# Token-list writes without order among themselves, and the early index reads moved ahead of the last batch's writes

## Chip, core and metric

The kernel runs on one core of a Trainium2 chip. The metric is the device time of one execution in microseconds (us); three runs of the kernel before are known, and their median is compared with the median of the changed kernel. The engines are named as in the profile: PE (matmul), PEld (its weight load), DVE (VectorE), ACT (ScalarE), POOL (GpSimd), SP (SyncE, which here only issues transfers). SPq and POOLq are the sequencers of SP and POOL.

## What is computed

Attention in two steps, a dense layer, and a mixture of eight experts of which every token takes one:

```python
p_packed = sm_attn(p, k, v)                    # 8 batches, 8 heads, 576 tokens, head_dim 64
x = sm_attn(q, p_packed, p_packed)             # -> x of shape (4608, 512)
h = x @ w_in ; x = (h - tanh(h)) @ w_out       # w_in 512x2048, w_out 2048x512
logits = x @ w_gate                            # 8 experts
e_idx = argmax(logits, axis=1)
for e in range(8):
    mask = e_idx == e
    ye = relu(x[mask] @ w1[e]) @ w2[e]         # w1 512x1024, w2 1024x512
    out[mask] = gate_w[mask, None] * eom[mask, e, None] * ye
```

## The kernel before

A first part packs keys and values. Then 16 half batches of 288 tokens (`halves`) go through attention and the dense layer, one after the other on PE: `up` (first matrix), `up_b`, `down` (second matrix), 16 steps `f` each. What belongs beside this is put into a table by `at(i, f, function)`: it is emitted in the program behind step `f` of half batch `i`, and every engine works its share strictly in that order. So (15, 4) is behind step 4 of the last half batch, and calls with the same place keep the order in which they were entered.

While half batch `i` is on PE, the half batch before it is routed: `logits` to `rank` find each token's expert and its rank there; `place` (15 of 16 at step 5; the last one after the loop) computes where each token stands in its expert's list and writes the token numbers to `tab`, a table in DRAM with 4608 places for each expert. It does so with three indirect transfers from POOL (L610), 96 numbers of four bytes each, after DVE has made the addresses `ix` (L608). One step later `gate_b` scales the rows and sends them from `x2s` to `x2d` in DRAM by four transfers from SP (L634).

When the last half batch is under way, the expert with most tokens so far is known (`favour`), and its weights are fetched (`early_fetch`, `early_split`). Its first three tiles of 128 tokens are the early tiles 0, 1, 2. `gather` brings a tile in: SP loads the tile's offset (L783), then reads 128 token numbers from `tab` into `ixt` (L785); POOL gathers the 128 rows from `x2d` into `xg` (L788), for which there are two buffers. `early_gather` for tiles 0 and 1 stands at (15, 8), and for tile 2 at (15, 14) behind `x_up` of tile 0, in which PE transposes `xg` (L815). The reads take only lists that `place` had filled up to the half batch before.

After the loop, PE works the early tiles (`mm1`, `h_up`, `mm2`) while the last half batch is routed and placed. `listing` then makes the offsets `of_i` (L920) of all other tiles ("m" 0, 1, ...) on DVE; `gather` of tile m0 follows, and `x_up` of m0 stands in PE's order behind `mm2` of tile 1. A tile's result is copied to `y` (L865, one buffer) and written out by an indirect transfer from POOL (L867). Every tile up to the end is worked in this order; the weights of an expert that changes are fetched by `refetch` and split by `resplit`, both under a condition.

Of the kernel before, what the change touches and what calls it, by code (L numbers as in the profile page):

```python
# [8 lines left out]
F32 = mybir.dt.float32  # L9
# [3 lines left out]
U32 = mybir.dt.uint32  # L13
# [6 lines left out]
NB, NH, S, D = 8, 8, 576, 64  # L20
# [3 lines left out]
NT = NB * S  # L24
# [5 lines left out]
EARLY = 3  # L30
# [14 lines left out]
def attention_moe_kernel(ctx: ExitStack, tc: tile.TileContext, q, k, v, p, w_in, w_out, w_gate, w_og, w1, w2, out):  # L45
    nc = tc.nc
    vec, act, pool, pe, sp = nc.vector, nc.scalar, nc.gpsimd, nc.tensor, nc.sync
# [3 lines left out]
    tab = dram.tile([TROWS, 1], I32, name="tab")  # L51
# [3 lines left out]
    def open_pool(name, bufs=1, side="left", space=None):  # L55
        kw = {"space": space} if space is not None else {"side": side}
        kw["reuse_waits"] = "tile"
        pl = tc.alloc_tile_pool(name=name, bufs=bufs, **kw)
        pools.append(pl)
        return pl  # L60
# [6 lines left out]
    const = open_pool("const")  # L67
# [2 lines left out]
    base_e = const.tile([1, NE], F32, name="base_e")  # L70
    iota_e = const.tile([1, NE], F32, name="iota_e")
    quad = const.tile([128, 1], F32, name="quad")

    ef = open_pool("ef")
    w_in_sb = ef.tile([128, 4, DFF], F32, name="w_in_sb")
# [8 lines left out]
    tok = cab.tile([96, 2 * NB, 3], I32, name="tok")  # L84
# [228 lines left out]
    with ExitStack() as pa:  # L313
# [107 lines left out]
        for a in range(4):  # L421
            r = slice(32 * a, 32 * a + 32)
# [53 lines left out]
    with ExitStack() as pb:  # L476
# [117 lines left out]
        def place(b, hf):  # L594
            n = HB * NE
            pr_, oh = tmp["pr"], tmp["oh"]
            vec.tensor_copy(seg[:, :, 1:], pr_[:, n:2 * n].rearrange("p (t e) -> p e t", e=NE))
            so = tmp['rt'].tile([128, NE, HB + 1], F32, name="so")
            vec.tensor_tensor_scan(so.rearrange("p e t -> p (e t)"), smask.rearrange("p e t -> p (e t)"), seg.rearrange("p e t -> p (e t)"), 0.0, ALU.mult, ALU.add)
            pos = tmp['rt'].tile([128, HB, NE], F32, name="pos")  # L600
            vec.tensor_tensor(pos, pr_[:, :n].rearrange("p (t e) -> p t e", e=NE), so[:, :, 0:HB].rearrange("p e t -> p t e"), op=ALU.add)
            vec.tensor_copy(seg[:, :, 0:1], so[:, :, HB:HB + 1])
            vec.tensor_tensor(pos, pos, oh, op=ALU.mult)
            ps = tmp['rt'].tile([128, HB], F32, name="ps")
            vec.tensor_reduce(ps, pos, axis=AX.X, op=ALU.add)
            ix = tmp['rt'].tile([96, 3], I32, name="ix")
            for r in range(3):
                vec.tensor_copy(ix[32 * r:32 * r + 32], ps[32 * r:32 * r + 32, 3 * r:3 * r + 3])  # L608
            for j in range(3):
                pool.indirect_dma_start(tab, bass.IndirectOffsetOnAxis(ap=ix[:, j:j + 1].bitcast(U32), axis=0), tok[:, 2 * b + hf, j:j + 1], None)  # L610

        def gate(b, hf):
            oh, ex, lg = tmp["oh"], tmp["lex"], tmp["lg"]
# [26 lines left out]
        def at(i, f, fn, *a):  # L640
            i, f = divmod(NF * i + f, NF)
            todo.setdefault((i, f), []).append((fn, a))
# [11 lines left out]
        for i, (b, hf) in enumerate(halves):  # L654
            n = b + 1
            if i:
                p_ = halves[i - 1]
                at(i, 0, logits)
                at(i, 1, logits_b)
                at(i, 2, choose_a)  # L660
                at(i, 3, choose_b)
                at(i, 4, rank)
                at(i, 5, place, *p_)
                at(i, 5, gate, *p_)
                at(i, 6, gate_b, *p_)
# [37 lines left out]
        st = {}  # L703
# [75 lines left out]

        plain = {0, 1, 2, ("m", 0), ("m", 1)} | {("m", n) for n in range(NMAIN + 2, NSTEP)}  # L780

        def gather(key, off, rows=NT + 1):
            r = sp.value_load(off, min_val=0, max_val=TROWS - 128)  # L783
            ix = const.tile([128, 1], I32, name="ixt", bufs=6)
            sp.dma_start(ix, tab[bass.ds(r, 128)].rearrange("(j g) o -> g j o", g=4))  # L785
            xg = st["cg"].tile([128, 4, 128], F32, name="xg", bufs=2)
            if key in plain:
                pool.indirect_dma_start(xg.rearrange("p c n -> p (c n)"), None, x2d[:rows], bass.IndirectOffsetOnAxis(ap=ix.bitcast(U32), axis=0))  # L788
            else:
                iq = const.tile([128, 4], I32, name="iq", bufs=3)  # L790
                sp.dma_start(iq, tab[bass.ds(r, 128)].rearrange("(j g) o -> j (g o)", g=4).unsqueeze(0).broadcast_to([4, 32, 4]))
                pool.tensor_scalar(iq, iq, 4.0, quad, op0=ALU.mult, op1=ALU.add)
                src = x2d[:rows].rearrange("n (q c) -> (n q) c", q=4)
                for g in range(4):
                    pool.indirect_dma_start(xg[:, g], None, src, bass.IndirectOffsetOnAxis(ap=iq[:, g:g + 1].bitcast(U32), axis=0))  # L795
            st["g", key] = xg, ix

        def early_gather(n):
            gather(n, st["eo"][:, n:n + 1], NT - S)

        def open_gather():
            close(rt)
# [177 lines left out]
        for n, f in enumerate((13, 15, 17, 19, 20, 23, 26, 28)):  # L980
            if n < 2:
                at(14, 10, early_fetch, n)
            at(14, f, early_split, n)
            if n + 2 < 8:
                at(14, f, early_fetch, n + 2)
        at(15, 7, open_gather)
        at(15, 8, early_gather, 0)
        at(15, 8, early_gather, 1)
# [82 lines left out]
        for n in range(NMAIN):  # L1071
            s = n % 2
            key = "m", n
# [20 lines left out]
        for n in range(NMAIN, NSTEP):  # L1094
            key = "m", n
# [48 lines left out]
```

## Time and profile before

| | |
|---|---|
| median of 3 runs | 1365.23 us (1360.34 to 1365.89) |
| profiled execution: its time / its span | 1369.21 us / 1367.3 us |
| mean granted clock of TensorE in it | 0.963 of full speed |
| PE busy | 1265.3 us, 93% of the span |
| PEld busy | 1082.4 us, 79% |
| DVE busy | 816.1 us, 60% |
| ACT busy | 530.1 us, 39% |
| POOL busy | 327.9 us, 24%, 363 instructions |

PE is the busiest engine, and in the page's forty slices it is busy for nine tenths or more from the seventh to the thirty-ninth, with one gap: two slices of 8 and 6 tenths, somewhat behind the middle of the span. That gap is where the half batches end and the early tiles begin. Busy time is an average over stages; the rows further down show what PE waits for in that gap.

### The profile page before, as it was taken

How to read it: one execution, taken by the hardware profiler on the slowest of the kernel's cores; microseconds unless marked ns; L12 is line 12 of the kernel's file. 1: busy time of each engine (PE TensorE's matmuls, PEld its weight loads, DVE VectorE, ACT ScalarE, POOL GpSimd, SP SyncE). 2: the span in 40 equal slices, each digit the busy share in tenths (PEclk: the TensorE clock that was granted, in tenths of full speed). 3: DMA queues.
4: the chain of work that ended last, by engine and by line, in shares of the span. 5: the costliest groups of instructions: out<-in, count | busy, mean ns of one | idle time of the engine just before them, and what ended most of it. 6: DMA issues, size and time to landing. Idle time of an engine off the chain costs nothing. (4 is left out here: it accounts for less than half of the span.)

```text
span 1367.3 us, 25742 instructions
## 1 busy us (share of the span) xinstructions
PE 1265.3 (93%) x9024; PEld 1082.4 (79%) x9024; DVE 816.1 (60%) x1811; ACT 530.1 (39%) x1141; POOL 327.9 (24%) x363
## 2 busy tenths in 40 slices
PE   6575879999999999999999999869999999999997
PEld 5354668998989989889899899757888778788775
DVE  3755996777776777768677777363233533443551
ACT  4555434443434344343434435332222422332431
POOL 3313760000000000000000000115444444454431
PEclk7878889999999999999999999989999999999999
DMA  8999421122111221122103023331113311332441
GB/s 227 242 246 207 138 64 22 15 36 36 27 19 27 36 30 24 19 36 36 26 11 53 19 47 112 117 80 39 44 47 101 105 46 45 113 100 73 131 154 41
DMA packets 140354, 102.24 MB, mean 75 GB/s; under 512 B 97296, under 2 KB 121876, under 8 KB 139572
## 3 DMA queue, kind: packets, MB, share of 16 engines
q1 hardware_dynamic: 130516, 80.33, 25.5%
q0 software_dynamic: 9696, 20.14, 4.8%
q8 instruction: 74, 1.21, 0.4%
q14 instruction: 68, 0.56, 0.2%
HBM read 215.60 MB, written 19.57 MB: 172 GB/s over the span
## 5 line engine op out<-in xcount | busy, mean ns | idle before, releaser
L610 POOL DMA_INDIRECT tab<-tok,ix x48 | 45.3, 943 | 641.5 <-DVE ix L608 460.7
L517 ACT ACTIVATE gh<-gg 128x288 fp32r<-128x288 f32 x256 | 112.6, 440 | 153.2 <-PE acc L532 68.0
L518 DVE TENSOR_TENSOR gl<-gg,gh 128x288 fp32r<-128x288 f32 x244 | 109.9, 450 | 96.9 <-ACT gh L517 90.6
L531 PE MATMUL acc<-gl,wo_bt 128*128 128x288 f32 x512 | 154.9, 303 | 11.5 <-DVE gl L518 7.0
L851 DVE TENSOR_TENSOR hl<-pt,hh 128x512 fp32r<-128x512 f32 x76 | 52.3, 690 | 185.4 <-ACT hh L850 174.2
L504 PE MATMUL ph<-a_hi,wf_hi 128*128 128x288 f32 x512 | 160.5, 314 | 0.9 <-DVE gg L510 0.5
L506 PE MATMUL ph<-a_hi,wf_lo 128*128 128x288 f32 x512 | 152.7, 298 | 3.9 <-DVE wf_lo L228 3.9
L531 PE MATMUL acc<-gl,wo_a 128*128 128x288 f32 x512 | 152.8, 298 | 3.7 <-POOL gl L518 3.7
L795 POOL DMA_INDIRECT xg<-x2d,iq x132 | 138.4, 1049 | 64.5 <-issue 57.0
L530 PE MATMUL acc<-gh,wo_a 128*128 128x288 f32 x512 | 152.1, 297 | 1.8 <-ACT pp L298 1.8
L532 PE MATMUL acc<-gh,wo_bt 128*128 128x288 f32 x512 | 152.8, 298 | 0.0
L530 PE MATMUL acc<-gh,wo_bt 128*128 128x288 f32 x512 | 152.7, 298 | 0.0
L505 PE MATMUL ph<-a_lo,wf_hi 128*128 128x288 f32 x512 | 152.3, 297 | 0.0
L532 PE MATMUL acc<-gh,wo_a 128*128 128x288 f32 x512 | 152.3, 297 | 0.0
L510 DVE TENSOR_TENSOR gg<-ph,th 128x288 f32<-128x288 f32 x256 | 115.9, 453 | 55.6 <-ACT th L508 54.3
L839 ACT ACTIVATE h<-ph 128x512 f32<-128x512 f32 x76 | 45.3, 598 | 241.1 <-PE ph L838 205.3
L508 ACT ACTIVATE th<-ph 128x288 f32<-128x288 f32 x256 | 104.1, 406 | 78.8 <-PE ph L506 77.7
L504 PEld LDWEIGHTS ph<-a_hi,wf_hi 128*128 128x128 f32 x512 | 97.3, 190 | 43.4 <-issue 38.6
L860 PE MATMUL py<-w2h,hh 128*128 128x512 f32 x304 | 127.0, 418 | 0.2
L861 PE MATMUL py<-w2l,hh 128*128 128x512 f32 x304 | 121.1, 398 | 1.7 <-DVE w2l L765 1.7
L837 PE MATMUL ph<-w1l,xh 128*128 128x512 f32 x304 | 121.2, 399 | 1.4 <-DVE w1l L765 1.0
L862 PE MATMUL py<-w2h,hl 128*128 128x512 f32 x304 | 120.8, 397 | 0.0
(223 smaller groups left out, 2756.8 us busy)
## 6 DMA issues: line engine op xcount, KB each, us to landing
raw<-in_moe_w_dram SPq DMA_DIRECT2D x37, 2048.0 KB
sraw<-in_moe_w_dram SPq DMA_DIRECT2D x37, 1024.0 KB
x2s<-in_moe_w_dram SPq DMA_DIRECT2D x37, 1024.0 KB
kt<-in_k_dram SPq DMA_DIRECT2D x16, 576.0 KB
vt<-in_v_dram SPq DMA_DIRECT2D x48, 192.0 KB
x2d<-x2s SPq DMA_DIRECT2D x64, 144.0 KB
qt<-in_q_dram SPq DMA_DIRECT2D x240, 36.0 KB
st<-in_moe_w_in_dram SPq DMA_DIRECT2D x16, 512.0 KB
```

The lines of the kernel that those rows point to most:

```text
L504: pe.matmul(ph, lhsT=wf_hi[n][:, g, c], rhs=ah[:, g], start=g == 0, stop=False)
L505: pe.matmul(ph, lhsT=wf_hi[n][:, g, c], rhs=al[:, g], start=False, stop=False)
L506: pe.matmul(ph, lhsT=wf_lo[n][:, g, c], rhs=ah[:, g], start=False, stop=g == 1)
L510: vec.tensor_tensor(gg, ph, th, op=ALU.subtract)
L530: pe.matmul(acc[j], lhsT=hi[:, j], rhs=gh, start=f == 0, stop=False)
L531: pe.matmul(acc[j], lhsT=hi[:, j], rhs=gl, start=False, stop=False)
L532: pe.matmul(acc[j], lhsT=lo[:, j], rhs=gh, start=False, stop=f == NF - 1)
L795: pool.indirect_dma_start(xg[:, g], None, src, bass.IndirectOffsetOnAxis(ap=iq[:, g:g + 1].bitcast(U32), axis=0))
L837: pe.matmul(ph, lhsT=xh[:, c], rhs=w1l[:, c, r], start=False, stop=False)
L860: pe.matmul(py, lhsT=hh[:, c], rhs=w2h[:, c], start=c == 0, stop=False)
L861: pe.matmul(py, lhsT=hh[:, c], rhs=w2l[:, c], start=False, stop=False)
L862: pe.matmul(py, lhsT=hl[:, c], rhs=w2h[:, c], start=False, stop=c == 7)
```

## The change

Two things are changed. The 48 transfers that write `tab` are declared free of order among themselves, each with a one-element `memset` of a scratch tile ahead of it on POOL; a read of `tab` is made to wait for all writes that came before it in the program. And the offsets and token numbers of the three early tiles are read by `early_index` at (15, 4), ahead of the `place` at (15, 5), and no longer inside `early_gather`, which only gathers now.

```diff
+    gap = const.tile([1, 1], F32, name="gap")
...
             for j in range(3):
-                pool.indirect_dma_start(tab, bass.IndirectOffsetOnAxis(ap=ix[:, j:j + 1].bitcast(U32), axis=0), tok[:, 2 * b + hf, j:j + 1], None)
+                pool.memset(gap, 0.0)
+                apart(pool.indirect_dma_start(tab, bass.IndirectOffsetOnAxis(ap=ix[:, j:j + 1].bitcast(U32), axis=0), tok[:, 2 * b + hf, j:j + 1], None))
+
+        listed = []
+
+        def apart(ins):
+            ins = ins.ins
+            if listed:
+                tc.declare_no_dep(ins, group="tab", reason="places of their own")
+            tc.add_to_no_dep_group("tab", ins)
+            listed.append(ins)
+
+        def read_list(ins):
+            for m in listed:
+                tc.add_manual_dep(ins.ins, m.name, mybir.DependencyInfo(mybir.DependencyClass.Sync, mybir.DependencyReason.DATA), reason="all places are written")
+            listed[:] = []
...
-        def gather(key, off, rows=NT + 1):
+        def early_index(n):
+            st["r", n] = read_index(st["eo"][:, n:n + 1])
+
+        def read_index(off):
             r = sp.value_load(off, min_val=0, max_val=TROWS - 128)
             ix = const.tile([128, 1], I32, name="ixt", bufs=6)
-            sp.dma_start(ix, tab[bass.ds(r, 128)].rearrange("(j g) o -> g j o", g=4))
+            got = sp.dma_start(ix, tab[bass.ds(r, 128)].rearrange("(j g) o -> g j o", g=4))
+            if listed:
+                read_list(got)
+            return r, ix
+
+        def gather(key, off, rows=NT + 1):
+            r, ix = read_index(off) if off is not None else st["r", key]
...
         def early_gather(n):
-            gather(n, st["eo"][:, n:n + 1], NT - S)
+            gather(n, None, NT - S)
...
+        for n in range(EARLY):
+            at(15, 4, early_index, n)
         at(15, 7, open_gather)
         at(15, 8, early_gather, 0)
```

How the instructions stand on the two engines that issue these transfers follows, in the program's order. A wait on DMASW or DMAHW is one for a transfer from POOL or from SP, on one of eight counters that are used in turn; DVE, PE and Pool are waits for those engines.

On POOL, before, around the `place` of the last half batch but one (the first three lines), the early gathers, and the last `place`:

```order
L610 DMA tab<-tok,ix 36992x1 [waits DMASW3_49,DVE_49]
L610 DMA tab<-tok,ix 36992x1 [waits DMASW4_49]
L610 DMA tab<-tok,ix 36992x1 [waits DMASW5_49]
L788 DMA xg<-x2d,ixt 128x512 [waits DMAHW4_49,DMAHW3_49,DMAHW5_49,DMAHW2_49,DMAHW6_49,DMAHW1_49,DMAHW7_49,DMAHW0_49,Activation_49]
...
L788 DMA xg<-x2d,ixt 128x512 [waits DMAHW2_49,DMASW7_49,PE_49]
...
L610 DMA tab<-tok,ix 36992x1 [waits DMASW6_49,DVE_49]
L610 DMA tab<-tok,ix 36992x1 [waits DMASW2_49]
L610 DMA tab<-tok,ix 36992x1 [waits DMASW3_49]
L788 DMA xg<-x2d,ixt 128x512 [waits DMAHW5_49,DMAHW1_49,DMAHW6_49,DMAHW0_49,DMAHW7_49,DMASW0_49,PE_49]
L867 DMA out_dram<-y,ixt 4608x512 [waits DVE_49]
```

The same place on POOL in the changed kernel:

```order
L612 DMA tab<-tok,ix 36992x1 [waits DMAHW3_49,DMAHW4_49,DMASW4_49,DMAHW5_49,DMASW3_49,DVE_49]
L611 MEMSET gap 1x1 [waits Pool_49]
L612 DMA tab<-tok,ix 36992x1 [waits DMASW5_49]
L611 MEMSET gap 1x1 [waits Pool_49]
L612 DMA tab<-tok,ix 36992x1 [waits DMASW6_49]
L814 DMA xg<-x2d,ixt 128x512 [waits DMAHW2_49,DMAHW1_49,DMAHW6_49,DMAHW0_49,DMAHW7_49,DMASW7_49,Activation_49]
...
L612 DMA tab<-tok,ix 36992x1 [waits DMASW2_49,DVE_49]
L611 MEMSET gap 1x1 [waits Pool_49]
L612 DMA tab<-tok,ix 36992x1
L611 MEMSET gap 1x1 [waits Pool_49]
L612 DMA tab<-tok,ix 36992x1 [waits DMASW4_49]
L814 DMA xg<-x2d,ixt 128x512 [waits DMAHW1_49,DMAHW5_49,DMAHW0_49,DMAHW6_49,DMASW5_49,DMAHW7_49,DMASW0_49,PE_49]
```

Before, the second and third write each wait for the counter of the write just ahead of them. Afterwards a write that names a DMASW counter names that of a transfer of an earlier half batch or tile, since the counters go round; the first write of the last half batch but one now also waits for the three index reads (DMAHW3 to 5).

On SP, before, from the second last weight fetch of the early tiles to the first index read:

```order
L760 DMA sraw<-in_moe_w_dram 128x2x512 [waits DMAHW2_49,DMAHW0_49,DVE_49]
L634 DMA x2d<-x2s 32x9x128 [waits DMAHW3_49,DVE_49]
L634 DMA x2d<-x2s 32x9x128 x3
L760 ISA
L760 DMA sraw<-in_moe_w_dram 128x2x512 [waits DMAHW1_49,DVE_49]
L783 TENSOR_LOAD eo [waits DVE_49]
L783 ISA x2
L785 REGISTER_ALU
L785 DMA ixt<-tab 128x1x1 [waits DMASW6_49,DMASW0_49]
```

And in the changed kernel:

```order
L777 DMA sraw<-in_moe_w_dram 128x2x512 [waits DMAHW2_49,DMAHW0_49,DVE_49]
L803 TENSOR_LOAD eo [waits DVE_49]
L803 ISA x2
L805 REGISTER_ALU
L805 DMA ixt<-tab 128x1x1 [waits DMASW5_49,DMASW4_49,DMASW6_49,DMASW3_49,DMASW7_49,DMASW2_49,DMAHW3_49,DMASW1_49,DMASW0_49]
...
L651 DMA x2d<-x2s 32x9x128 [waits DVE_49]
L651 DMA x2d<-x2s 32x9x128 x2
L651 DMA x2d<-x2s 32x9x128 [waits DMAHW1_49]
L777 ISA
L777 DMA sraw<-in_moe_w_dram 128x2x512 [waits DMAHW2_49,DVE_49]
```

The three loads and index reads (the other two read the same but for their waits and are left out) now stand ahead of the row transfers of the last half batch but one, and the first of them waits for all writes of the list up to the half batch before that.

## Rows read from the trace of the kernel before

**Rows 1.** Timeline of PE: start, length in us, instruction; in brackets idle before, and releaser.

```profile
868.88 1.10 PE L815 MATMUL px<-ident,xg 128*128 128x128 f32 x4 [4.75 <-DMA xg<-x2d,ixt]
...
916.90 1.13 PE L815 MATMUL px<-ident,xg 128*128 128x128 f32 x4 [10.32 <-DMA xg<-x2d,ixt]
...
934.22 0.39 PE L838 MATMUL ph<-w1h,xl 128*128 128x512 f32 x1
```

**Rows 2.** Stretches: length, busy PE, PEld, DVE, ACT, POOL, granted clock, DMA share, GB/s.

```profile
868.00:874.60 6.60, 5.72 (x21) 5.36 (x22) 2.53 (x5) 2.25 (x5) 1.76 (x5) 0.50 0.50 122
...
908.90:922.30 13.40, 5.40 (x15) 4.20 (x16) 2.43 (x3) 4.11 (x5) 4.00 (x4) 0.50 0.44 157
966.00:978.00 12.00, 12.00 (x58) 9.86 (x57) 3.90 (x6) 2.92 (x5) 4.95 (x6) 1.00 0.16 45
```

**Rows 3.** Waits of SP's queue, 835 to 862 and then 895 to 912: total, times, longest.

```profile
SPq L785 <- DMA tab<-tok,ix: 9.6, 1, 9.6
...
SPq L634 <- DVE gl L518: 6.8, 1, 6.8
...
SPq L785 <- DMA tab<-tok,ix: 5.8, 1, 5.8
```

**Rows 4.** Timeline of SP: transfers as issued.

```profile
848.48 2.02 SPq L634 DMA_DIRECT2D x2d<-x2s  x4
...
862.01 4.59 SPq L785 DMA_DIRECT2D ixt<-tab  x3
...
905.75 0.64 SPq L785 DMA_DIRECT2D ixt<-tab  x1
```

**Rows 5.** Instructions of L785 on SP, 895 to 912: ns min/median/max, first and last start.

```profile
L785 SPq MOVE ixt<-tab x2: 29/34/38, 899.9 to 909.7; - x2
```

**Rows 6.** Timeline of POOL: its transfers.

```profile
639.53 0.91 POOL L610 DMA_INDIRECT tab<-tok,ix  x1 [8.96 <-DMA tab<-tok,ix]
...
844.70 0.92 POOL L610 DMA_INDIRECT tab<-tok,ix  x1 [25.14 <-DVE ix L608]
849.33 1.77 POOL L610 DMA_INDIRECT tab<-tok,ix  x1 [3.72 <-DMA tab<-tok,ix]
857.62 0.92 POOL L610 DMA_INDIRECT tab<-tok,ix  x1 [6.51 <-DMA tab<-tok,ix]
865.31 0.99 POOL L788 DMA_INDIRECT xg<-x2d,ixt  x1 [6.78 <-DMA ixt<-tab]
...
889.76 0.93 POOL L610 DMA_INDIRECT tab<-tok,ix  x1 [18.18 <-DVE ix L608]
894.19 0.93 POOL L610 DMA_INDIRECT tab<-tok,ix  x1 [3.50 <-DMA tab<-tok,ix]
900.99 0.91 POOL L610 DMA_INDIRECT tab<-tok,ix  x1 [5.87 <-DMA tab<-tok,ix]
910.49 0.99 POOL L788 DMA_INDIRECT xg<-x2d,ixt  x1 [8.60 <-issue]
911.79 1.01 POOL L867 DMA_INDIRECT out_dram<-y,ixt  x1 [0.31 <-issue]
913.11 0.98 POOL L788 DMA_INDIRECT xg<-x2d,ixt  x1 [0.30 <-issue]
```

**Rows 7.** Groups of POOL by line: busy us, mean ns, idle before.

```profile
L395 POOL MEMSET quad<- 32x1 f32 x4 | 0.4, 92 | 0.1
```

**Rows 8.** Timeline of DVE.

```profile
904.79 2.34 DVE L765 TENSOR_TENSOR w1l<-raw,w1h 128x1024 fp32r<-128x1024 f32 x2
...
918.43 0.69 DVE L865 COPY y<-py 128x512 f32<-128x512 f32 x1 [10.11 <-DMA out_dram<-y,ixt]
...
925.88 0.69 DVE L865 COPY y<-py 128x512 f32<-128x512 f32 x1 [5.01 <-PE py L862]
...
927.62 2.36 DVE L765 TENSOR_TENSOR w2l<-x2s,w2h 128x1024 fp32r<-128x1024 f32 x2
...
933.08 0.68 DVE L823 TENSOR_TENSOR xl<-px,xh 128x512 fp32r<-128x512 f32 x1
```

## The prediction

> **What bounds the kernel now.** I read the timeline of PE first, because PE is the busiest engine. In the second half it waits long at two places only, both the transpose that opens a tile: 4.75 us before early tile 0, and 10.32 us before tile m0, each released by the gather of `xg` [rows 1]. [...] The two waits therefore cost about 4.75 + 2.86 = 7.6 us and 10.32 + 2.70 = 13.0 us. Further on PE has no room: in the row from 966 to 978 it is busy for all 12.00 us at clock 1.00 [rows 2], and the order of the work there does not depend on the list's writes. I take it that what PE gains at the two places reaches the end.
>
> Then the chain behind each wait. POOL's timeline shows the three writes of a half batch in a row, each behind the landing of the one before: 844.70, 849.33, 857.62, and 889.76, 894.19, 900.99 [rows 6]. SP's own waits show who stands behind them: the index read of early tile 0 waited 9.6 us for the writes, that of m0 5.8 us [rows 3]. The reads went out at 862.01 and 905.75 [rows 4], the gathers at 865.31 and 910.49 [rows 6], and PE went on at 868.88 and 916.90.
>
> **The first wait.** The three early reads no longer stand behind the writes of the last half batch but one. They go into SP's queue after a weight fetch, ahead of the row transfers of 848.48. There SP waited 6.8 us for DVE before those transfers [rows 3], that is from about 841.7. Three reads with the two loads between them took 4.59 us, 0.64 of it the last read [rows 4]; so read and load take (4.59 - 0.64) / 2 = 1.98 us, a load alone 1.3, and the three with the first load 5.9 us, inside the 6.8. If that cover were gone, the row transfers would go out late by the excess.
>
> The reads push the first write on POOL, which now waits for them. The third read goes out at about 847; from a read's issue to the gather that uses it took 3.30 us in one case and 4.74 in the other [rows 4, 6], so the writes start at 850 to 852 and not at 844.70, and the third is issued by 855. Nothing reads the list between there and the last half batch. The gather of tile 0 stands next on POOL. Its buffer lies where the routing scratch was, so it still waits for the row transfers of 848.48 to land. That landing has no row; the list write of 849.33, which ran beside them, landed at 857.62 [rows 6], and I take that. Gather at 857.6, PE can go on 3.57 us later (865.31 to 868.88), at 861.2. PE arrives at 868.88 - 4.75 = 864.1. So this wait goes, with 2.9 us in hand, and with it the slow clock: **7.6 us**.
>
> All that follows depends on PE through the drain and the routing, and moves forward by these 7.6 us. I go on in the times of the trace before and add the two gains at the end.
>
> **The second wait.** The writes start at 889.76 as before. From one to the next I count 0.93 us for the write, 0.30 us of issue (the bracket of 913.11), 0.09 for the memset [rows 7], and nothing to 0.3 us for a second issue gap: 1.3 to 1.6 us. So the third ends between 893.3 and 893.9, not at 901.90. It lands 3.85 us later if it behaves like the third write now (901.90 to 905.75), and 5.87 us later if like the second, which ran beside row transfers [rows 6]: 897.2 to 899.8, or 901.0 at most if it is held as long as the second write was (900.99). SP had the offset of m0 ready at 899.9 [rows 5] and waited from there. The read therefore goes out at 899.9 to 901.0: the wait of 5.8 us nearly goes, and what is late next is the offset itself, at the end of DVE's `listing`. The gather follows by 3.30 or 4.74 us, at 903.2 to 905.7, and PE 3.57 us after it, at 906.8 to 909.3. The 6.41 us that this gather took (910.49 to 916.90) I don't take: it shared the DMA engines with a weight fetch which SP issues two steps later, and in the new order the rows are there before it. I take 908.0. PE arrives at 916.90 - 10.32 = 906.6, so 1.4 us of wait are left. Before, the clock fell 2.3 us after PE had gone idle (908.9 against 906.6); I take it that it doesn't fall, and keep 2.7 us for the case that it does.
>
> What is late next behind that? From 916.90 to the third matmul of tile m1 (934.22) PE took 17.32 us; without the slow clock 14.6. It would come at 921.4 to 923.9, taking 922.6. But this matmul needs `xl`, and DVE's order ahead of it holds the copies of `y`, which has one buffer, so each copy waits for the write-out of the tile before. Now the copy of tile 1 waits 10.11 us for such a write [rows 8]; the copy of tile 2 did not, only because PE came so late. The write-out of tile 1 stands on POOL behind the gather of m1. That gather's read stands on SP behind `refetch`, whose staging tile DVE frees at 907.1 [rows 8]: read at about 908 at the earliest, gather 3.3 us later at 911.4, and 913.11 as now at the latest. Write-out of tile 1 at 912.7 to 914.4. It lands after 4.63 us (a list write, 844.70 to 849.33) to 6.64 us (tile 0's, 911.79 to 918.43): 917.3 to 921.0. From the copy of tile 2 DVE needs 4.10 us to the end of the weight splits (925.88 to 929.98), 0.68 each for one `hl` and for `xl`, and PE 0.46 us more: 923.2 to 926.9. I take 5.3 us for the landing, since the weight fetch should be mostly through, and the middle of the starts: 924.7. That is later than PE's own 922.6, so this copy, not the gather, sets the place. Gain: 934.22 - 924.7 = **9.5 us**.
>
> **The other parts.** The 48 memsets are 48 x 0.09 = 4.4 us on POOL, which idles 18 to 25 us ahead of the writes of a half batch [rows 6]; without that cover they would cost those 4.4. In the first 14 half batches the writes bunch together, and nobody waits for them. The extra wait of the first early read is for writes some 20 us old.
>
> **Sum.** 7.6 + 9.5 = 17.1 us. Span 1367.3 to 1350.2; the profiled execution 1369.21 to 1352.1. That execution lies 4 us above the median of the runs, so from 1365.23 it is **1348.1 us**. A measurement here tells about 0.5% (6.8 us) from no change.
>
> **Rivals.**
> *Writes in flight together land late* (13%). Second writes, which run beside the row transfers, took 5.87, 6.51 and up to 8.96 us to land, first ones 3.50 and 3.72 [rows 6]. At 8.96 the third lands at 902.7; read, gather and PE follow to 909.6 to 911.0; the clock falls, 2.7 us; the matmul of m1 comes at 926.9 to 928.3, the gain there is 5.9 to 7.3, and the time about 1351. If they slow each other so that the third lands at 905.75 as now, only 7.6 us are left: 1357.6. Against it: the third write's data is small, and the wait of 5.87 still fits.
> [...]
>
> *The first wait stays* (6%). It needs the gather of tile 0 later than 860.5: the row transfers would have to land 2.9 us after 857.6, for instance pushed by the three writes that now run beside them. Fully kept, only 9.5 us are gained: 1355.7.
>
> *Slower: POOL holds DVE up* (4%). In each of the 16 half batches the second and third write now come while DVE does the gating chain on which the next `gl` waits. If DVE stood still while POOL issues, that is 2 x 0.92 us, 16 times, 29 us against 17.1: about 1377. It decides from 17.1 / 16 = 1.07 us each. Against it: where a write ran beside a large DVE operation it was the write that took longer, 1.77 for 0.92 us (849.33) [rows 6].
> [...]
>
> *The change does nothing* (3%). The counters that the writes still name belong to transfers at least two half batches or tiles back, so I hardly believe it: 1365.
>
> **The numbers.** The forecast has 74%. Its own range: 7.6 plus 7.3 to 12.8 (matmul at 926.9 to 921.4, the latter if the copy of `y` doesn't bind), so 1344.8 to 1350.3. The runs of before spread from 4.9 below their median to 0.7 above, which takes the low end to 1342.5; the high end reaches into the first two rivals, 1355. Faster 0.90 (forecast, and the first two rivals but for their ends), same 0.06, slower 0.04.
>
> **What would show it.** Right: three writes 1.3 to 1.6 us apart; early reads at 842 to 848; no wait at `x_up` of tile 0 and clock 1.00 through 874; m0's read right behind its offset; a wait of 1 to 2 us at `x_up` of m0; then a wait of about 2 us at `xl` of m1, behind a `y` copy that waits for a write-out. Wrong: a long landing of the third write, a gather of m0 that still takes 6.4 us, or a new wait of PE inside the half batches.

## The result, and the profile after

The changed kernel takes 1350.54 us (median of 18 runs, 1345.01 to 1361.54), the kernel before 1363.72 us beside it (18 runs, 1358.33 to 1365.89): the ratio is 0.9907, 95% interval 0.9893 to 0.9921. That is 13.2 us less, where 17.1 us were forecast. The profiled execution took 1349.53 us, its span 1347.6 us. Line numbers move: the list write L610 is now L612 (its memset L611), the row transfer L634 is L651, the index read L785 is L805, the gather L788 is L814, the transpose L815 is L841, `mm1`'s third matmul L838 is L864, the `y` copy L865 is L891.

The timeline of PE shows the two places of [rows 1] and the matmul of tile m1:

```profile
859.91 0.72 PE L841 MATMUL px<-ident,xg 128*128 128x128 f32 x4 [1.76 <-DMA xg<-x2d,ixt]
...
900.29 1.13 PE L841 MATMUL px<-ident,xg 128*128 128x128 f32 x4 [5.29 <-DMA xg<-x2d,ixt]
...
918.09 0.39 PE L864 MATMUL ph<-w1h,xl 128*128 128x512 f32 x1
```

The first wait fell from 4.75 to 1.76 us, the second from 10.32 to 5.29; neither is gone. The clock in stretches behind them (columns as in [rows 2]):

```profile
860.00:866.00 6.00, 6.00 (x38) 4.72 (x39) 2.17 (x5) 2.88 (x7) 1.35 (x5) 1.00 0.58 187
...
901.00:906.50 5.50, 5.28 (x14) 3.86 (x14) 1.94 (x3) 4.54 (x5) 1.96 (x2) 0.50 0.63 241
```

Behind the short wait the granted clock stays at 1.00; behind the longer it is at 0.50, as it was before.

The timeline of POOL, from the writes of the last half batch but one to the gather of m0 (compare [rows 6]):

```profile
844.17 0.96 POOL L612 DMA_INDIRECT tab<-tok,ix  x1 [41.04 <-DMA ixt<-tab]
845.43 0.91 POOL L612 DMA_INDIRECT tab<-tok,ix  x1 [0.22 <-issue]
846.65 0.91 POOL L612 DMA_INDIRECT tab<-tok,ix  x1 [0.22 <-issue]
847.87 1.00 POOL L814 DMA_INDIRECT xg<-x2d,ixt  x1 [0.30 <-PE ph L507]
...
878.17 0.93 POOL L612 DMA_INDIRECT tab<-tok,ix  x1 [15.91 <-DVE ix L609]
879.41 2.04 POOL L612 DMA_INDIRECT tab<-tok,ix  x1 [0.22 <-issue]
881.75 0.91 POOL L612 DMA_INDIRECT tab<-tok,ix  x1 [0.21 <-issue]
896.66 0.99 POOL L814 DMA_INDIRECT xg<-x2d,ixt  x1 [14.00 <-issue]
```

And that of SP over the same time (compare [rows 4]), with SP's own wait ahead of m0's index read:

```profile
837.07 4.56 SPq L805 DMA_DIRECT2D ixt<-tab  x3
842.50 2.04 SPq L651 DMA_DIRECT2D x2d<-x2s  x4
844.80 0.50 SPq L777 DMA_DIRECT2D sraw<-in_moe_w_dram  x1
...
880.68 1.85 SPq L651 DMA_DIRECT2D x2d<-x2s  x4
892.79 0.64 SPq L805 DMA_DIRECT2D ixt<-tab  x1
```

```profile
SPq L805 <- DMA tab<-tok,ix: 4.4, 1, 4.4
```

The writes follow each other at 1.2 to 2.3 us and the early reads stand ahead of them, as the change says. But the third write of the last half batch, off POOL at 882.66, holds SP until 892.79: it landed about 10.1 us after it had left POOL. Before, the third landed 3.85 us after (901.90 to 905.75). The table of transfers (count, KB where known, median us from issue to landing) points the same way. Its count is of all transfers, but its median only of those whose landing the trace gives: here five of the 48, four at 11.0 to 11.9 us and one, the first of its three, at 4.2, none of them in the last two half batches:

```profile
tab<-tok,ix POOLq DMA_INDIRECT x48, 11.4
```

and, asked for 842 to 862 alone, of the early gathers, where it knows the landing of one of the three, that of tile 0:

```profile
xg<-x2d,ixt POOLq DMA_INDIRECT x3, 11.9
```

Where the 13.2 us came in can be read from the lead over the trace of before (the time of an instruction there minus its time here). PE reaches the transpose of tile 0 at 868.88 - 4.75 = 864.13 before and 859.91 - 1.76 = 858.15 after: a lead of 5.98 us that was there ahead of both places. Nearly all of it is there at the first list write of the whole program, before and after:

```profile
225.92 1.04 POOL L610 DMA_INDIRECT tab<-tok,ix  x1 [23.87 <-DVE ix L608]
```

```profile
220.21 1.03 POOL L612 DMA_INDIRECT tab<-tok,ix  x1 [23.81 <-DVE ix L609]
```

Ahead of it the change adds no more than a memset, so this lead is hardly of its making; other kernels with all writes apart have from -7.2 to 5.1 us there. At the first write of the last `place` it is 889.76 - 878.17 = 11.59, at the matmul of m1 934.22 - 918.09 = 16.13, at the end 1367.3 - 1347.6 = 19.7. So the first place gave 5.6 us, the second 4.5, and 3.6 came later, where the forecast had nothing. Of these 3.6 some 1.5 are a wait of PE that the trace of before has and this one hasn't:

```profile
1098.07 0.66 PE L848 MATMUL pt<-ident,h 128*128 128x128 f32 x4 [1.53 <-ACT h L839]
```

Whether it went by the change or by the execution, no run shows. The profiled execution of before lies 1369.21 - 1363.72 = 5.5 us above its median and this one 1.0 below its own; 19.7 - 6.5 = 13.2.

The 4.5 us of the second place come only in small part from the writes. From the first of the three to the read behind them it is 14.62 us (878.17 to 892.79) where it was 15.99 (889.76 to 905.75), 1.4 us less. The gather leaves 3.87 us after the read and not 4.74, and PE goes on 3.63 us after the gather and not 6.41: 3.7 us. From there to m1 PE takes 0.5 us more. Every kernel below with the writes apart has 3.4 to 4.6 us from this gather to PE, the one with the writes in order 5.35; what shortens it wasn't tested.

### The profile page after: what moved, and what is told of

Its sections match the earlier page's. It is cut to its first block, busy times and chain, and to the rows that moved or that the text cites. A ratio compares the mean times of both kernels' runs of the same rounds, so it can differ in the third digit from the quotient of the medians.

```text
span 1347.6 us, 25792 instructions
## 1 busy us (share of the span) xinstructions
PE 1264.4 (94%) x9024; PEld 1083.4 (80%) x9024; DVE 815.7 (61%) x1811; ACT 530.3 (39%) x1141; POOL 340.1 (25%) x411
## 5 line engine op out<-in xcount | busy, mean ns | idle before, releaser
L612 POOL DMA_INDIRECT tab<-tok,ix x48 | 53.4, 1113 | 614.1 <-DVE ix L609 566.1
L865 ACT ACTIVATE h<-ph 128x512 f32<-128x512 f32 x76 | 45.4, 598 | 237.9 <-PE ph L864 237.9
```

## Experiments

Twelve kernels, in four rounds on four chips; each is compared with the kernel before of its own round. The ratio with its interval is the one on record for all runs of both; it isn't the quotient of the two medians. Two chips ran that kernel at 1368 to 1369 us (rounds 1 and 2), two at 1362 us (rounds 3 and 4). "Tile 0" and "m0" are PE's waits at the two places in us; the gains are leads worked out as above, from the arrival at tile 0 to the first write of the last `place`, and from there to the matmul of m1.

| round, kernel | median us | ratio, interval | tile 0 | m0 | gain 1 | gain 2 |
|---|---|---|---|---|---|---|
| the change, first comparison | 1350.54 | 0.9907, 0.9893 to 0.9921 | 1.76 | 5.29 | 5.6 | 4.5 |
| 1 early reads only | 1366.28 | 0.9976, 0.9956 to 0.9996 | 6.54 | 8.78 | -1.7 | 2.5 |
| 1 writes apart only | 1362.46 | 0.9942, 0.9922 to 0.9963 | none | 4.40 | 7.4 | 6.8 |
| 1 rows behind the list | 1359.48 | 0.9938, 0.9913 to 0.9962 | 0.30 | 5.28 | 7.1 | 5.0 |
| 1 gathers first | 1362.98 | 0.9963, 0.9941 to 0.9985 | none | 4.72 | 7.4 | 6.8 |
| 2 the change again | 1360.02 | 0.9943, 0.9924 to 0.9963 | none | 4.69 | 7.4 | 5.9 |
| 2 rows last | 1358.78 | 0.9937, 0.9913 to 0.9961 | none | 3.90 | 7.4 | 5.9 |
| 2 gathers first, rows last | 1368.22 | 0.9992, 0.9978 to 1.0006 | none | 3.91 | 5.0 | 6.0 |
| 2 fourth write | 1362.71 | 0.9968, 0.9948 to 0.9989 | 0.38 | 4.47 | 7.0 | 5.8 |
| 3 last six writes apart | 1350.94 | 0.9906, 0.9883 to 0.9930 | 1.33 | 4.75 | 6.0 | 6.8 |
| 3 the same, rows last | 1349.01 | 0.9910, 0.9879 to 0.9941 | 1.00 | 3.81 | 6.4 | 5.6 |
| 3 the same, gathers first | 1352.88 | 0.9930, 0.9908 to 0.9952 | none | 4.58 | 7.4 | 6.9 |
| 4 last six writes apart, again | 1350.62 | 0.9922, 0.9900 to 0.9943 | 1.38 | 3.84 | 5.9 | 7.7 |

My theory after the result (A): what was mis-sized is the landing of the list's writes; with several in flight, beside row transfers, they land late, and a gather behind them in POOL's queue lands late too. The rivals (B) are in each expectation.

### Which of the two edits does it

**Early reads only.** The list's writes are plain again, without memset:

```diff
-                pool.memset(gap, 0.0)
-                apart(pool.indirect_dma_start(tab, ...))
+                pool.indirect_dma_start(tab, ...)
```

> The early index reads stay ahead of the writes, but the list's writes are in order again, as before the change. Times are those of the changed kernel's trace, in which PE reaches the transpose of early tile 0 at about 858.2 and the writes of the last half batch but one start at 844.2. Theory A (a gather lands behind the list writes that stand ahead of it in POOL's own DMA queue, whether they are ordered or not): the three writes are again issued some 4.6 and 8.3 us apart, the third at about 857; gather 0 follows at 858 to 859 and its rows land at 862 to 864, so PE waits 4 to 6 us there, the clock falls, and nothing is gained at the first place. The second place is as before the change too (10 us of wait). Total gain 0 to 2 us, ratio 0.998 to 1.000. Theory B (the early reads alone take the first wait away): PE waits under 1 us at early tile 0, 5.7 us or more are gained, ratio 0.995 to 0.996.

The timeline of POOL, and PE's row at tile 0:

```profile
862.14 0.91 POOL L611 DMA_INDIRECT tab<-tok,ix  x1 [3.88 <-DMA tab<-tok,ix]
863.36 0.99 POOL L813 DMA_INDIRECT xg<-x2d,ixt  x1 [0.30 <-DVE gg L511]
```

```profile
871.64 1.10 PE L840 MATMUL px<-ident,xg 128*128 128x128 f32 x4 [6.54 <-DMA xg<-x2d,ixt]
```

Theory A, a little over its 4 to 6 us: the gather stands in POOL's order behind the third ordered write, and PE waits 6.54 us, more than the 4.75 before. The early reads alone gain nothing at the first place. (At the second, where this kernel does as the one before, its lead still grew by 2.5 us: so much can differ there from one execution to another, and gains at m0 are to be read with that.) That an index is ready early is of no use here while the gather that takes it is issued behind the writes.

**Writes apart only.** The index reads go back into the early gathers:

```diff
         def early_gather(n):
-            gather(n, None, NT - S)
+            gather(n, st["eo"][:, n:n + 1], NT - S)
...
-        for n in range(EARLY):
-            at(15, 4, early_index, n)
```

> The list's writes stay without order, but the index reads of the early tiles are back with their gathers, behind the writes of the last half batch but one. Theory A (three writes in flight together land 8 to 11 us after issue, about when they landed in order): the third write of that half batch lands at about 856.5 in the changed kernel's times, the first index read waits for it as before, and PE waits 4 to 5 us at early tile 0 with the slow clock behind it: no gain at the first place. At the second place the gain of the changed kernel remains, 4 to 5 us. Ratio 0.996 to 0.998. Theory B (they land 3.85 to 5.87 us after issue, as I forecast): the first read goes out at about 851 to 852, the gather at 855, PE doesn't wait at the first place, and the ratio is that of the change, 0.990 to 0.992.

Theory A had the first wait stay; it went altogether, and its place gave 7.4 us. The reason is a point that A left out: on this chip PE came later than I had reckoned (its transpose of tile 0 starts at 867.51; the idle times behind that are told further down). The gather went out at 863.48 and needed no more. What B says of the writes isn't right either: the first index read went out at 860.09, 8.8 us after the third write had ended (851.30), not at 851 to 852. So the writes' part alone does nearly what the whole change does on the same kind of chip (0.9942 against 0.9943).

### What holds the gather of tile 0

**Gathers first.** The writes of the last half batch but one go behind the gathers of tiles 0 and 1:

```diff
+            if hold:            # (b, hf) == (NB - 1, 0); ix is kept in a tile of its own
+                st["hold"] = ix
+            else:
+                write_list(b, hf, ix)
...
         at(15, 8, early_gather, 0)
         at(15, 8, early_gather, 1)
+        at(15, 8, write_list, NB - 1, 0)
```

> The three list writes of the last half batch but one are issued on POOL behind the gathers of early tiles 0 and 1, and no longer ahead of them; nobody reads that part of the list before the last half batch. In the changed kernel the gather of tile 0 was issued at 847.87 and its rows landed at 859.8, 12 us later, and PE waited 1.76 us. Theory A (the gather's packets stand behind those of the list writes in POOL's own queue): the gather goes out at 847 or a little later, when its buffer is free, its rows land 4 to 7 us after that, PE's wait of 1.76 us at early tile 0 is gone, and 1.8 us are gained against the changed kernel. Theory B (the weight fetch and the row transfers beside it fill the DMA engines): the gather still takes 10 us or more and the wait of 1 to 2 us stays. In both the second place is as in the changed kernel.

The wait is gone, but the change again, on a chip of the same kind, has none either, since PE comes late there. Round 3 tells more: there the kernel without this edit waits 1.33 us and the one with it not at all. The transfers issued from 840 to 880, with their median from issue to landing, without the edit and then with it (all landings are known in the first pair, two of three in each row of the second):

```profile
tab<-tok,ix POOLq DMA_INDIRECT x3, 9.9
xg<-x2d,ixt POOLq DMA_INDIRECT x3, 9.5
```

```profile
xg<-x2d,ixt POOLq DMA_INDIRECT x3, 6.0
tab<-tok,ixl POOLq DMA_INDIRECT x3, 6.7
```

One by one: without the edit the three writes of 848.33 to 850.91 land at 856.9 to 860.8, and the gathers of tiles 0 and 1 behind them at 863.6 and 864.2, which is 11.5 and 9.5 us after issue; that of tile 2, issued at 864.74 when the writes had landed, takes 3.3 us. With the edit the gather of tile 0 takes 5.5 us, and that of tile 2, issued at 864.99 and now behind the writes, 6.5. Tile 0 alone doesn't rule B out, for with the edit its gather leaves 1.2 us ahead of the row transfers (847.35 against 848.59). Tile 2 does, since its gather has the same transfers from SP around it in both kernels: what makes the gathers late is their place behind the list writes (A). The median of the whole program is not better for it: 1362.98 in round 1, 1352.88 in round 3, within the intervals of the kernels beside it or above.

### What holds the third write

**Rows behind the list.** The first row transfer of the last half batch waits for its three writes:

```diff
+                if (b, hf) == (NB - 1, 1) and g == 0:
+                    for m in listed: tc.add_manual_dep(sent.ins, m.name, ...)
```

> The first of the four row transfers of the last half batch waits until the three list writes of that half batch have landed; nothing else is changed against the changed kernel. In that kernel the third write was issued at 881.75, beside the row transfers of 880.68, and landed at 892.6, 11 us later. Theory A (the row transfers, whose packets share the DMA engines, are what holds the third write up): without them beside it the third lands by 886 to 888, 4 to 6 us after issue, the index read of m0 goes out behind it or behind the offsets (887.5), and the row transfers then take their turn, landing 8 to 11 us after 888; the rows bound the gather, PE goes on at 896 to 899.6, 1 to 4 us earlier than the 900.29. Theory B (three scattered writes in flight hold each other up): the third still lands at about 892, the row transfers go out only then and land at about 900, and PE waits some 8 us longer: the time is 1 to 1.5% nearer to the kernel before, ratio 0.996 to 0.998.

Neither: the rows left SP at 897.38, behind a third write that had ended at 889.61, so it landed 7.8 us after with no rows beside it. With rows beside it these were 9.4 us in the same round (writes apart only), 9.3 in the change again (890.28 to 899.60, below) and 10.1 in the first trace: the rows are worth 1.5 to 2.3 us of it. The rest is there with the three writes alone. Round 3 shows it with the DMA engines otherwise empty: in its kernel "the same, rows last" the rows leave SP only at 887.75. The packets from 879 to 882, those from 882 to 887.7, and the third write, issued at 880.19:

```profile
DMA packets 96, 0.00 MB, mean 0 GB/s; under 512 B 96, under 2 KB 96, under 8 KB 96
```

```profile
DMA packets 1, 0.01 MB, mean 1 GB/s; under 512 B 0, under 2 KB 0, under 8 KB 0
```

```profile
tab<-tok,ix POOLq DMA_INDIRECT x1, 8.4
```

The 96 packets of the three writes have been moved by 882, then one packet, of the program's own instructions, is all that moves, and the third write lands at 888.6, 8.4 us after its issue. Before the change the third write, alone, took 4.8 (900.99 to 905.75). The wait at m0 stays at 5.28, because the read now stands behind the rows on SP (900.45).

**Rows last.** The offsets ahead of the rows' scaling:

```diff
-        gate_b(*last)
         x_up(2)
         listing()
+        gate_b(*last)
```

> The offsets of the tiles are made ahead of the scaling of the last half batch's rows on DVE, so the four row transfers leave later, behind the three list writes and not beside them. Numbers in times of the changed kernel's first trace. Theory A (the three list writes take their turn, 8.5 us from the issue of the third with nothing beside them, as with the rows held back): the third lands at about 890.2 and not 892.6; the index read follows behind it, but the rows, sent at 886 to 888, land at 894 or later and bound the gather: PE goes on at 897.5 to 898.5, wait 2.5 to 3.5 us, 2 to 3 us gained. Theory B (the rows beside them are what holds the writes up): the third lands at 886.5, the rows at 891.7, PE goes on at 895.3, the wait is under 1 us and the clock doesn't fall, 7 to 8 us gained.

Between the two: PE waits 3.90 us, near A's range; the rows went only at 895.08, since DVE works `listing` first, and the read behind them at 898.36. B is out: the clock fell again (mean 0.52 of full speed from 905 to 912). The rows, with no list write beside them, moved in stretches at

```profile
895.30:897.30 2.00, 1.58 (x10) 1.35 (x10) 1.93 (x6) 1.88 (x3) 0.00 (x0) 1.00 0.62 121
897.30:899.30 2.00, 2.00 (x12) 1.59 (x11) 1.97 (x8) 1.10 (x2) 0.00 (x0) 1.00 0.76 174
899.30:901.30 2.00, 2.00 (x12) 1.68 (x11) 2.00 (x3) 0.60 (x1) 0.00 (x0) 1.00 0.03 0
```

(last column GB/s): all 4 x 144 KB in some 4.5 us. In the changed kernel, in its first trace, beside three writes:

```profile
880.90:883.90 3.00, 3.00 (x15) 2.41 (x14) 2.62 (x15) 1.87 (x2) 1.55 (x3) 1.00 0.98 149
883.90:886.90 3.00, 3.00 (x15) 2.49 (x14) 2.83 (x10) 0.60 (x1) 0.00 (x0) 1.00 0.74 51
886.90:889.90 3.00, 3.00 (x17) 2.48 (x16) 2.86 (x10) 1.35 (x2) 0.00 (x0) 1.00 0.00 0
889.90:892.90 3.00, 3.00 (x16) 2.44 (x16) 2.96 (x8) 2.23 (x4) 0.00 (x0) 1.00 0.00 0
```

The bytes have moved by 886.9 (149 x 3 + 51 x 3 = 600 KB). Then the DMA engines show a busy share of 0.00 for 6 us, and all that time the third write is outstanding; SP, which has m0's offset from 888.4 on, waits for it until 892.79. So it is not bandwidth that is short in these 6 us; what the writes wait for there, no view shows.

**Fourth write.** Between the second and the third a further write, of the second's numbers, into a table of its own:

```diff
+                if (b, hf, j) == (NB - 1, 1, 2):
+                    pool.indirect_dma_start(tab2, ... ix[:, 1:2] ..., tok[:, 2 * b + hf, 1:2], None)
+                    pool.memset(gap, 0.0)
```

> A fourth list write of the last half batch, between the second and the third, of the second's numbers into a second table that nobody reads; the third is issued one write and one memset (1.2 us) later. Theory A (the scattered writes of 96 numbers take their turn in POOL's queue, 2.5 to 3.5 us each): the third write lands 2.5 to 3.5 us later than in the changed kernel, the index read of m0 goes out that much later, PE waits 7.5 to 9 us at m0. Theory B (a fixed delay from issue to landing, however many are in flight): everything moves by 1.2 us and PE waits 6.5 us.

```profile
889.95 0.92 POOL L616 DMA_INDIRECT tab<-tok,ix  x1 [0.23 <-issue]
```

```profile
899.60 0.64 SPq L809 DMA_DIRECT2D ixt<-tab  x1
```

The third write ended at 890.87 and the read went 8.7 us later; in the change again these were 890.28 and 9.3. From the first write's start to the read it is 14.45 against 13.80 us; but the kernels with three writes and the rows beside them have 13.5 to 14.6 for this, so no cost of the fourth write can be told from their spread. A as I had put it (each takes its turn, 2.5 to 3.5 us) falls; B's 1.2 us aren't excluded, though PE's wait was 4.47, less than either theory had. The read leaves 11.0 to 12.1 us after the first of them was issued in every one of these kernels in which the rows stand beside the writes (880.68 to 892.79 at first; 888.30 to 899.60 and 887.66 to 899.60 in round 2). But in all of them the rows leave 2.5 us behind the first write, so this doesn't tell the rows from the writes.

The rows beside the third write are worth 1.5 to 2.3 us; the 7.8 us of three writes with no rows beside them show that the rows are only a part of it. Why three list writes in flight land later than one alone stays open.

### Less of the one, and both edits together

**Gathers first and rows last**, the two edits above in one kernel.

> The two edits together: list writes of the last half batch but one behind the gathers of early tiles 0 and 1, and the offsets ahead of the scaling of the last half batch's rows. Theory A: no wait at early tile 0 (7.6 us against the kernel before at the first place, as with that edit alone), a wait of 2.5 to 3.5 us at tile m0; 4 to 5 us faster than the changed kernel of the same chip. Theory B (the wait that is taken away at the first place comes back at the second, since the list then is written later and PE comes earlier): nothing gained against the changed kernel.

No wait at tile 0 and 3.91 us at m0: the waits are a little above A's; but 1368.22 us in the median, no better than the kernel before. The profile is of little use for where that went, since its execution is 8.8 us above the median (1376.97) and lies 7.2 us behind the trace of before at the first list write of the program already. It stays open, and I don't recommend the pair.

**The change again.**

> The changed kernel once more, on the chip of the runs beside it. In the three variants of it that were run before (writes apart only, rows behind the list, gathers first) ACT stood idle for some 2 to 3 us near 678, beside smaller idle times in the half batches, which its first profile doesn't show, and those runs gained 0.4 to 0.6% and not 0.9%. Theory A (that loss belongs to the chip or the execution): here it shows in the changed kernel too, and the ratio is 0.994 to 0.997. Theory B (it belongs to the variants): the profile shows none of it and the ratio is 0.989 to 0.992 again. The waits at the two places are as in its first profile in both: 1 to 2 us at early tile 0, 5 to 6 us at tile m0.

Theory A. The ratio is 0.9943 and not 0.9907, though the two places give 7.4 and 5.9 us. The rest is lost in the half batches: the lead over the trace of before is 5.1 us at the first list write of the program (220.8) and -1.7 at the one of 806.2. PE's busy time there, 225 to 840, in the change's first trace, in the change again, and in the kernel of round 1 with ordered writes:

```profile
225.00:840.00 615.00, 607.50 (x4828) 552.68 (x4828) 446.57 (x1176) 256.60 (x629) 47.26 (x78) 1.00 0.30 33
```

```profile
225.00:840.00 615.00, 603.23 (x4775) 546.13 (x4775) 440.75 (x1157) 252.49 (x624) 47.19 (x78) 1.00 0.27 31
```

```profile
225.00:840.00 615.00, 607.65 (x4837) 552.07 (x4837) 447.56 (x1178) 255.99 (x631) 38.63 (x42) 1.00 0.18 32
```

In all seven kernels of rounds 1 and 2 with all writes apart PE is busy for 603.2 to 605.0 us of these 615. One place is in the timeline of ACT, the change again and then ordered writes; it is the same instruction, for which the matmuls were done in both (in the change again at 677.1, 2.9 us before it starts):

```profile
680.03 0.41 ACT L509 ACTIVATE th<-ph 128x288 f32<-128x288 f32 x1 [3.25 <-PE px L221]
```

```profile
679.13 0.41 ACT L509 ACTIVATE th<-ph 128x288 f32<-128x288 f32 x1 [0.41 <-PE ph L507]
```

**Last six writes apart**, all others in order again:

```diff
-                apart(pool.indirect_dma_start(tab, ...))
+                put = pool.indirect_dma_start(tab, ...)
+                if b == NB - 1:
+                    apart(put)
```

> Only the six writes of the last two half batches are without order; the 42 before them are in order again, each with its memset. Early index reads as in the changed kernel. On the chip of the last two rounds the changed kernel falls back against the kernel before by 6.8 us between 269 and 711, inside the half batches (its lead goes from 5.1 to -1.7 us at 842), with idle times of ACT of 1.5 to 4 us for which its inputs were ready; the kernel with ordered writes and early reads shows none of it there (from -2.0 to -1.0). Theory A (the writes in flight together cause it): without them there no loss, the lead is held through the half batches, and the ratio is 0.988 to 0.991, 5 to 7 us better than the 0.9943 of the changed kernel. Theory B (it comes from the chip or the layout, not from these writes): the loss of 5 to 7 us stays and the ratio is 0.993 to 0.996. Should this round run on a chip like that of the first comparison, where the changed kernel had no such loss, both give 0.990 to 0.992.

> The kernel with only the last six writes apart, and with the offsets ahead of the scaling of the last half batch's rows. Theory A (second place as in the run of that edit alone, where PE waited 3.9 us and not 4.7 us at m0): 1 us better than the kernel with the last six writes apart, ratio 0.987 to 0.990. Theory B (the half batches lose as before): 0.993 to 0.995.

> The kernel with only the last six writes apart, and with the list writes of the last half batch but one behind the gathers of early tiles 0 and 1. Theory A (first place as in the run of that edit alone, where the whole 7.6 us came in): 1.5 to 2 us better than the kernel with the last six writes apart, ratio 0.987 to 0.990. Theory B (what that edit wins in its profile is lost elsewhere, as its median of 0.9963 suggests): not better than it.

> The kernel with only the last six writes apart, once more, since its first round ran on a chip where the kernel before takes 1362 us, at which the changed kernel had no loss in the half batches either. On a chip where the kernel before takes 1368 us: Theory A (the unordered writes cause the idle times of ACT) 0.988 to 0.991 and no loss between 269 and 711; Theory B (chip or layout) 0.993 to 0.996 and a loss of 5 to 7 us there. On a chip at 1362 us it says nothing of this and gives 0.989 to 0.992 again.

Both rounds fell on chips at 1362 us, where the theories agree, and 0.9906 and 0.9922 are what both give. PE is busy for 607.6 to 607.7 us from 225 to 840 in all four. So the question stays open: on the chip of round 1 the order of the writes makes the difference (607.65 with order, in one trace, 604.3 to 604.7 without, in three), and on the chip of the first comparison it makes none (607.50 without). What ACT waited for, no view shows. What these kernels do show is that 42 of the 48 unordered writes are worth nothing for the gain on such chips: six are enough. They also show the landing with order, in the table of transfers of the first of them (42 of 48 in order; 41 landings known, 36 of them of writes in order), beside the 11.4 of the change:

```profile
tab<-tok,ix POOLq DMA_INDIRECT x48, 6.1
```

In order, the first of three takes 4.0 to 5.0 us, the second, beside the row transfers, 7.1 to 9.2, the third 4.4 to 6.7. In the change the one first write that is known takes 4.2, two second ones 11.4 and 11.9, two third ones 11.0 and 11.6.

Of their variants, rows last (1349.01) and gathers first (1352.88) lie on both sides of 1350.94, within what the rounds can tell; none is shown to beat the change.

## Why the prediction was right, and where it was not

The time was in the range and the sign was right; the sum, 17.1 us, was 3.9 us too much. That the time itself missed by only 2.4 us (1350.54 against 1348.1) is in part luck: at the two places 10.1 us came in, 7.0 less than forecast; 3.6 came later where the prediction had nothing, and the kernel before came out 1.5 us below the median that I started from. The range, 1342.5 to 1355, also took in the first rival, whose "about 1351" is nearer to what was measured than the forecast. By its steps:

- *PE's two waits bound, and what is gained there reaches the end.* Right: 5.6 + 4.5 us came in at the two places, and no lead was lost behind them (3.6 more came, of which the cause isn't shown). The 2.86 and 2.70 us for the slow clock are half of the 5.72 and 5.40 us of PE work at clock 0.50 [rows 2]; that this work takes twice as long as at 1.00, no run shows. In the change's trace matmuls of 512 columns start 0.43 us apart at 0.50 (902.63 to 906.04) and 0.23 us apart at 1.00 (941.65 to 947.02), 1.83 times as long; by that I estimate 2.6 and 2.4 us. Where the first wait went wholly, the place gave 7.4 us, 2.65 beyond the wait of 4.75.
- *Three writes 1.3 to 1.6 us apart.* Nearly: 1.2 us, and 2.3 where the second ran beside DVE's scaling of the rows and took 2.04 us.
- *The first wait goes wholly, 7.6 us: gather at 857.6, rows at 861.2, 2.9 us in hand.* Off. The gather went out sooner than I had it (847.87, which is 853.9 in the times of the trace before; I held its buffer until 857.6), but its rows took 12.0 us and not 3.57: it stood behind the three list writes. The wait left is 1.76 us, with no slow clock; 5.6 of 7.6 us came in. With the gather ahead of the writes 7.4 came in.
- *The third write lands 3.85 to 5.87 us after its end, at 897.2 to 901.0.* This is the step that failed. It landed 10.1 us after (892.79, which is 904.4 in the times of the trace before), 7.8 with no row transfers beside it; taking the order away brought the read only 1.4 us nearer to the first write. I had taken the landing from writes that each had the queue for themselves [rows 6], and the change's point was that they no longer do. The first rival, *writes in flight together land late* (13%), describes what happened; it reckoned 8.96 us and a gain of 5.9 to 7.3 us here, and 4.5 came in (5.6 to 7.7 in the kernels that wait 3.8 to 4.8 us at m0).
- *The offset is late next, the read right behind it.* It was not: SP had the offset 4.4 us ahead of the read.
- *The gather of m0 takes 3.57 us and not 6.41.* Right: 3.63. With the read following the writes so little sooner, this is the largest part of what the second place gave.
- *A wait of 1.4 us, and the clock doesn't fall.* 5.29 us, and it fell: 0.50 from 901.0 to 906.5, with 5.28 us of PE work in it. So the 2.7 us kept for that case were due, 2.4 of them by the estimate above.
- *Then a copy of `y` binds.* Not reached in the change, since PE comes too late for it. In the kernel with the last six writes apart the copy of tile 2 does wait for a write-out, 1.42 us, and PE waits for neither.
- *The memsets cost nothing, and POOL doesn't hold DVE up.* On the chip of the first comparison, right: PE's busy time in the half batches is 607.50 us with them. On two other chips the half batches lose 2.6 to 4.4 us of it with unordered writes, in the one place that is shown at ACT; that I did not foresee, and its cause stays open.

## To carry to other kernels

A landing time read from transfers that wait for each other doesn't hold once they overlap: here the group of three without order took 13.5 to 14.6 us from its first issue to the read behind it, where it took 15.6 and 16.0 in order. Take the landing of the group, and expect a gather behind it in the same queue to land no sooner than the group does: with the last six writes apart the writes landed at 856.9 to 860.8 and the gathers behind them at 863.6 and 864.2. Order on the queue that issues counts as much as dependence: put ahead of writes that nobody reads yet, the gather of tile 0 cost PE no wait where it cost 1.33 us behind them, though no median here is shown to be the better for it. And take order away where somebody waits for it; of 48 writes, six were enough here.

## What the runs showed of the hardware

- Scattered writes of 96 numbers of four bytes landed 4.0 to 9.2 us after issue, 6.1 in the median, when each waited for the one before (36 of one trace); in flight three at a time the second and third took 8.4 to 11.9. While the last was awaited the DMA engines showed a busy share of 0.00 for 6 us.
- From the first of three to the read behind them such a group took 13.5 to 14.6 us without order (15.6 and 16.0 with it); with a fourth write in it, 14.45.
- A gather of 128 rows landed 9.5 to 11.9 us after issue behind three such writes that hadn't landed, and 3.3 us (tile 2, last six writes apart) and 4.0 us (m1, the change) once they had.
- Four row transfers of 144 KB moved at up to 174 GB/s alone and at 51 GB/s in the second part of their time beside three list writes.
- The same program gained 0.9% on one chip and 0.6% on another, where ACT was idle for 3.25 us at an instruction whose inputs were done.
